# Linear attention feeding a residual MLP: load order of w_tok, its transposes, and the shape of the first q.kv products

## The chip, the cores and the metric

The kernel runs on one core of one Trainium2 chip. The metric is the device time of one execution in microseconds (us), taken as the median of several executions. The core has a matrix engine (TensorE, PE in the profile, its weight loads PEld), a vector engine (VectorE, DVE), a scalar engine (ScalarE, ACT), GpSimd (POOL), SyncE (SP), which here only issues transfers, and 16 DMA engines.

## The reference

Eight heads of linear attention are normalised, laid side by side as 512 channels, and go through a token-mixing and a channel-mixing layer:

```python
# q, k, v: (8, 8, 576, 64) fp32
kv  = np.einsum('bhsd,bhse->bhde', k, v)
o   = np.einsum('bhsd,bhde->bhse', q, kv)
o   = o / np.sqrt(np.mean(o * o, axis=-1, keepdims=True) + 1e-06) * g_norm
x   = o.transpose(0, 2, 1, 3).reshape(8, 576, 512)

a1  = alpha1 * x + beta1
tok = np.einsum('ts,bsd->btd', w_tok, a1)        # w_tok: (576, 576)
u   = x + lam * tok
a2  = alpha2 * u + beta2
ch  = np.maximum(a2 @ w_ch1, 0.0) @ w_ch2        # 512 -> 2048 -> 512
return u + lam * ch
```

## The kernel before

**A program that plans itself.** The code first lists all operations with what they read and write (`P.op`). Then `Prog.schedule` plays them through in planned time: each operation has a planned cost, each SP load a planned landing, and each engine takes, when it is free, the ready operation of lowest `pri`. Where an operation names several engines (a dict of costs), the planner chooses one. The result is a fixed order of instructions for each engine, written with semaphore waits. On the chip every engine follows its list; nothing is reordered at run time. `hasten` gives all ancestors of the first expansion matmuls a `pri` below -980, so the prologue goes ahead of everything else. The loads of the prologue are issued by SP strictly in the order of the list `order`; a load that waits for its buffer holds back those behind it.

When the planner finds nothing for PE before the first expansion matmul, it puts in a warm-up matmul (L1333) on zeros. `idle` says how soon after one the next may follow.

**PSUM.** There are eight banks of 512 fp32. `ptile(n)` is a tile of one or two banks, and `place` picks the banks.

**Tokens.** Token s of the 576 is written as 9 x (s // 9) + c. Column c of nine gives 64 tokens, so a group of two columns fills 128 partitions; the ninth column gives a half-filled group, and those of two batches share a tile (`xtl`).

**Prologue, batch 0.** Heads come in two halves (k0, v0, q0 and k1, v1, q1). For each half:
- `kv_groups` (L590): k.v in fp32, 64x64 products, four at a time in the quarters of the array; copies to `kvr` in fp32r, with the same values in the lower and the upper 64 partitions;
- `qt_groups` (L558, L551): q transposed by PE into `qtr` and `qtrt`;
- `qkv_groups` (L680, `f32`): q.kv in fp32r. Two token columns lie in the two 64-partition halves of `qtr`; a product has 64 rows, and lower and upper halves alternate, each writing a PSUM bank of its own;
- the norm: square (L709), sum (L711), root (L714), reciprocal (L717), scaling into `xm` (L733); then `rt` = x * alpha1 * lam * g (L737) and x * g (L740).

Batch 1 takes the same fp32r path with all eight heads at once; the later batches take a bf16 path with a high and a low part (L670, L385).

**w_tok.** `wt_groups` needs w_tok transposed, with rows and columns in the order of the tokens above. Five row groups of w_tok are loaded (four of 128 rows, one of 64). `cast` (L1109 on) reads every ninth column of a group and writes 512 reordered bf16 columns, `cast_tail` the ninth column's 64. Four PE transposes a group (L1136) and five for the tail (L1158) follow, copies into `wt`, and `sums` (L1188): the row sums of w_tok, two rows of which stand in `wt` for beta1 * lam (constant rows, stored into `rt` by DMAs that ScalarE issues, L1052).

`tok_half` (L800) is the token mixing of batch 0 by half of the channels, with its residual sum at L811. `ut_first` (L832) transposes u for the first expansion matmuls (L932, then L901). From there PE runs through expansion (L901 for even batches, L916 for odd), contraction (L966), token mixing of the next batch (L766, and L779 for the last 64 tokens of two batches), with the attention of a later batch between. The 64 last rows of w_tok serve only L779.

**Weights.** `load_w` brings w1 in four pieces (w0 to w3) and w2 in four (w4 to w7) through three buffers `stg`; w1 is cast (L1254), w2 scaled by `lam` (L1267). `bias_groups` (L1211) multiplies beta2 with w1. Bk, Bv, Bq in `order` are the loads of batch 1. `params` prepares rows such as `e1_bc`; its transpose L1033 waits for alpha2 and beta2, which ScalarE's queue loads.

Of the kernel before, what the change touches and what calls it, by code (L numbers as in the profile page):

```python
# [36 lines left out]
class PTile:  # L37
# [4 lines left out]
    def __init__(self, prog, n):  # L42
        self.prog, self.n, self.bank, self.ops = prog, n, None, []

    def ap(self, parts=slice(0, 128)):
        return self.prog.ps[parts, self.bank:self.bank + self.n, :]
# [5 lines left out]
class Prog:  # L52
# [79 lines left out]
    def schedule(self):  # L132
# [25 lines left out]
        def place(tile, t):  # L158
            if tile.n == 2:
                c = [b for b in (0, 2, 4, 6) if bank_ok(b, t) and bank_ok(b + 1, t)]  # L160
                if not c:
                    return None
                return min(c, key=lambda b: max(bank_since(b), bank_since(b + 1)))
            c = [b for b in range(8) if bank_ok(b, t)]
            if tile.spare:
                c += [b for b in range(8) if owner[b] is not None and owner[b].spare]
                return max(c, key=lambda b: (owner[b] is not None and owner[b].spare, b),
                           default=None)
            if not c:
                return None  # L170
            return min(c, key=lambda b: (bank_ok(b ^ 1, t), bank_since(b)))
# [43 lines left out]
        while left:  # L215
            progressed = False
            for e, q in queues.items():
                while q and free[e] <= t + 1e-9:
# [5 lines left out]
                    if e == "PE" and cold > 1.2:  # L224
                        cands = ([o for o in q[:2 * self.pe_window] if not o.cold]
                                 + [o for o in cands if o.cold])
                    for o in cands:
                        if not ready(o, t):
                            continue
                        if port_free > t + 0.1 and shared(o, e):  # L230
# [11 lines left out]
                    if pick is None and e == "PE" and first and t >= idle:  # L242
# [5 lines left out]
                        if ready(pick, t):  # L248
                            left += 1
                            q.append(pick)  # L250
                            idle = t + (1.0 if t < 9 else 2.0) * pick.cost
# [12 lines left out]
                    for tile in pick.alloc:  # L264
                        tile.bank = place(tile, t)
                        for b in range(tile.bank, tile.bank + tile.n):
# [8 lines left out]
                    if pick.lat is not None:  # L275
                        if e == "SP":
                            dma_free = max(dma_free, t + (1.9 if t < 3 else 1.25)) + pick.lat
# [114 lines left out]
def bass_transnormer_attn__then__resmlp_affine_kernel(  # L392
# [15 lines left out]
    with ExitStack() as stack:  # L408
# [24 lines left out]
        with nc.sbuf_tensor("kvr", [128, NH, DH], F32R) as kvr, \  # L433
                nc.sbuf_tensor("qtrt", [128, NH, 128], F32R) as qtrt:
# [13 lines left out]
        wt = sb("wt", [128, 6, S], BF16)  # L448
        w1 = sb("w1", [128, 4, FF], BF16)
# [7 lines left out]
        wst = hst[:, 0:2880].rearrange("p (c s) -> p c s", c=5)  # L457
        wsb = hst[:, 2880:4480].bitcast(BF16).rearrange("p (c s) -> p c s", c=5)
        smask = hst[:, 4480:4544].bitcast(BF16)
# [82 lines left out]
        def qt_groups(b):  # L542

            def group(a, m):
# [23 lines left out]
                else:  # L568
                    o = qtrt[0:64, 4 * a:4 * a + 4, lo:lo + 64]
# [800 lines left out]
```

## Time and profile before

| | us |
|---|---|
| median of 4 runs | 369.08 |
| lowest, highest | 367.11, 370.59 |
| profiled execution: its time | 370.06 |
| profiled execution: its span | 368.2 |
| PE busy | 356.9 (97%) |
| PEld, DVE, ACT, POOL busy | 211.2, 204.2, 146.9, 122.6 |
| first expansion matmul (L932) starts | 36.1 |
| first contraction matmul (L966) starts | 64.4 |
| last product ends | 364.7 |

The span is what the profiler saw from the first instruction to the last; the execution's time holds a little more around it (370.06 - 368.2 = 1.9). The kernel has a prologue of 36 us, in which loads, w_tok and the attention of batch 0 lie beside each other on all engines, and a long part in which PE works without a break. A time saved in the prologue counts if PE can start its long part sooner and then finds its operands.

### The profile page before, as it was taken

How to read it: one execution, taken by the hardware profiler on the slowest of the kernel's cores; microseconds unless marked ns; L12 is line 12 of the kernel's file. 1: busy time of each engine (PE TensorE's matmuls, PEld its weight loads, DVE VectorE, ACT ScalarE, POOL GpSimd, SP SyncE). 2: the span in 40 equal slices, each digit the busy share in tenths (PEclk: the TensorE clock that was granted, in tenths of full speed). 3: DMA queues.
4: the chain of work that ended last, by engine and by line, in shares of the span. 5: the costliest groups of instructions: out<-in, count | busy, mean ns of one | idle time of the engine just before them, and what ended most of it. 6: DMA issues, size and time to landing. Idle time of an engine off the chain costs nothing.

```text
span 368.2 us, 7917 instructions
## 1 busy us (share of the span) xinstructions
PE 356.9 (97%) x3542; PEld 211.2 (57%) x3302; DVE 204.2 (55%) x305; ACT 146.9 (40%) x254; POOL 122.6 (33%) x100
## 2 busy tenths in 40 slices
PE   6999959999999999999999999999999999999996
PEld 4878736447764464447754554447754554447644
DVE  1376729975397259752676179743874189720021
ACT  1588216404852048305860059006740157007600
POOL 4478464670055002730183004820572005400000
PEclk9989989999999999999999999999999999999999
DMA  8998997008694669387937685477946710341023
GB/s 286 352 385 266 341 373 279 2 0 124 155 352 80 120 115 378 76 107 120 318 112 116 130 258 214 84 103 113 372 72 112 150 31 0 64 94 30 0 59 85
DMA packets 67558, 59.17 MB, mean 161 GB/s; under 512 B 45552, under 2 KB 45828, under 8 KB 67524
## 3 DMA queue, kind: packets, MB, share of 16 engines
q1 hardware_dynamic: 67440, 58.65, 60.1%
q8 instruction: 27, 0.44, 0.5%
q14 instruction: 7, 0.06, 0.1%
q10 hardware_dynamic: 84, 0.02, 0.0%
HBM read 38.60 MB, written 9.44 MB: 130 GB/s over the span
## 4 chain that ended last, share of the span: by engine, by line
PE 93%; POOL 1%; DMA 1%; issue 1%; DVE 1%; ACTq 0%; ACT 0%; POOLq 0%
PE ps L966 34%; PE ps L916 19%; PE ps L901 14%; PE ps L766 8%; PE ps L590 5%; PE ps L385 2%; PE ps L670 2%; PE ps L680 2%; DMA w<-in_moe_beta_dram 1%; PE ps L558 1%; PE ps L779 1%; PE ps L1333 1%; PE ps L932 1%; POOL rt L737 1%; POOL xm L740 1%
## 5 line engine op out<-in xcount | busy, mean ns | idle before, releaser
L966 PE MATMUL ps<-w,ht 128*128 128x512 bf16 (+1 forms) x592 | 129.0, 373 | 0.0
L890 ACT ACTIVATE ht<-ps,bias 128x640 bf16<-128x640 f32 (+2 forms) x101 | 74.9, 743 | 50.9 <-PE ps L916 37.2
L966 PEld LDWEIGHTS ps<-w,ht 128*128 128x128 bf16 x592 | 56.7, 98 | 64.5 <-issue 1.6
L916 PE MATMUL ps<-a2t,w 128*128 128x320 bf16 x512 | 71.5, 299 | 0.0
L740 POOL TENSOR_TENSOR xm<-xm,g_bc 128x1024 f32<-128x1024 f32 (+1 forms) x16 | 33.3, 2082 | 109.5 <-DVE rt L737 109.1
L916 PEld LDWEIGHTS ps<-a2t,w 128*128 128x128 bf16 x512 | 49.5, 98 | 20.1
L901 PE MATMUL ps<-a2t,w 128*128 128x512 bf16 x240 | 55.7, 383 | 0.0
L977 DVE TENSOR_TENSOR xm<-ps,xm 128x512 f32<-128x512 f32 (+1 forms) x33 | 22.0, 673 | 55.7 <-PE ps L966 55.6
L621 ACT ACTIVATE kvd<-ps 64x256 bf16<-64x256 f32 x24 | 9.1, 378 | 97.1 <-PE ps L590 96.9
L711 DVE TENSOR_REDUCE small<-sq 128x16 f32<-128x1024 f32 (+3 forms) x27 | 24.9, 930 | 22.8 <-ACT sq L709 22.6
L901 PEld LDWEIGHTS ps<-a2t,w 128*128 128x128 bf16 x240 | 22.8, 99 | 25.4 <-issue 0.6
L766 PE MATMUL ps<-rt,wt 128*128 128x512 bf16 x140 | 31.4, 379 | 0.0
L891 DVE TENSOR_SCALAR ht<-ps,bias 128x512 bf16<-128x512 f32 (+2 forms) x31 | 22.2, 724 | 12.6 <-PE ps L901 6.4
L522 POOL TENSOR_TENSOR qs<-qf,qs 128x512 bf16<-128x512 f32 x13 | 16.5, 1270 | 28.2 <-ACT qs L481 27.5
L709 ACT ACTIVATE sq<-ps 128x1024 f32<-128x1024 f32 (+3 forms) x27 | 21.2, 797 | 11.3 <-PE ps L385 8.2
L749 DVE TENSOR_TENSOR xm<-ps,xm 128x512 f32<-128x512 f32 x28 | 19.1, 689 | 8.7 <-PE ps L766 7.1
L590 PE MATMUL ps<-vf,kf 64*64 64x64 f32 x1152 | 20.1, 226 | 3.9 <-issue 3.9
L766 PEld LDWEIGHTS ps<-rt,wt 128*128 128x128 bf16 x140 | 13.7, 98 | 16.5
L590 PEld LDWEIGHTS ps<-vf,kf 64*64 64x64 f32 x1152 | 18.7, 141 | 7.2 <-issue 7.0
L977 DVE TENSOR_TENSOR xtl<-ps,xtl 128x512 f32<-128x512 f32 x4 | 2.8, 692 | 35.5 <-PE ps L966 35.5
L751 POOL TENSOR_TENSOR a2b<-xm,a_bc 128x512 bf16<-128x512 f32 x12 | 18.2, 1513 | 8.7 <-DVE xm L749 8.4
L733 DVE TENSOR_TENSOR xm<-ps,small 128x1024 f32<-128x1024 f32 (+1 forms) x18 | 19.7, 1096 | 0.2
(101 smaller groups left out, 339.8 us busy)
## 6 DMA issues: line engine op xcount, KB each, us to landing
stg<-in_moe_w_ch_dram SPq DMA_DIRECT2D x8, 1024.0 KB, 13.2
kf<-in_k_dram SPq DMA_DIRECT2D x7, 1152.0 KB, 6.1
vf<-in_v_dram SPq DMA_DIRECT2D x7, 1152.0 KB, 9.6
qf<-in_q_dram SPq DMA_DIRECT2D x7, 1152.0 KB, 11.0
out_dram<-xm SPq DMA_DIRECT2D x62, 128.0 KB, 2.4
kf<-in_k_dram SPq DMA_DIRECT2D x2, 576.0 KB, 5.5
vf<-in_v_dram SPq DMA_DIRECT2D x2, 576.0 KB, 7.1
qf<-in_q_dram SPq DMA_DIRECT2D x2, 576.0 KB, 8.6
```

Source lines behind the costliest of these rows:

```text
L590: m = e.matmul(t.ap(slice(64 * i, 64 * i + 64))[:, y, 64 * x_:64 * x_ + 64], kf[rows, x, c], vf[rows, x, c], start=(c == 0), stop=(c == 8) ...
L709: P.op("ACT", act_us(64 * m), lambda e: e.activation(both(sqv), raw(), ACT.Square), r=[t], w=[("sq", sqs)])
L711: P.op("DVE", dve_us(64 * m), lambda e: e.tensor_reduce(out=smv, in_=sqv, axis=AX.X, op=ALU.add), r=[("sq", sqs)], w=[("sm", sms)], pri=-20)
L733: P.op("DVE", dve_us(64 * m), lambda e: e.tensor_tensor(out=x3, in0=raw(), in1=inv(), op=ALU.mult), r=[t, ("sm", sms)], w=xk, pri=-200)
L740: P.op(dve_pool(64 * m) if b < 2 else "POOL", pool_us(64 * m), lambda e: e.tensor_tensor(out=x3, in0=x3, in1=gb, op=ALU.mult), r=xk + ["g" ...
L766: m = e.matmul(t.flat(), wt[:, sc if sc < 4 else 4 + b % 2, 128 * c:128 * c + 128], rt[:, rs(b, sc), :], start=(sc == 0), stop=(sc == 4))
L890: return e.activation(dst, src(), ACT.Relu, bias=bi)
L891: return e.tensor_scalar(out=dst, in0=src(), scalar1=bi, scalar2=0.0, op0=ALU.add, op1=ALU.max)
L901: m = e.matmul(t.flat(), w1[:, dj, 128 * fj:128 * fj + 128], a2t[:, dj, 0:512], start=(dj == 0), stop=(dj == 3))
L916: m = e.matmul(t.ap()[:, i, 0:320], w1[:, dj, 128 * fj:128 * fj + 128], a2t[:, dj, 320 * i:320 * i + 320], start=(dj == 0), stop=(dj == 3))
L966: m = e.matmul(t.flat()[:, 0:m_], ht[:, fj, 128 * c:128 * c + 128], w2[:, fj, lo:hi], start=(fj == 0), stop=(fj == 15))
L977: P.op("DVE", dve_us(m_), lambda e: e.tensor_tensor(out=x, in0=t.flat()[:, 0:m_], in1=x, op=ALU.add), r=[t] + keys, w=keys)
```

## The change

- **w_tok in three parts.** `wt_groups(r)` takes row groups 0 and 1, then 2 and 3, then the last 64 rows. The loads t1 and t2 go later in `order`, t2 far later, into buffers of its own (`wst4`, `wsb4`). Token mixing waits for the part that it reads.
- **Plain casts.** `cast` writes 576 columns in their own order, `cast_tail` is gone. The column picks move to PE: weights are read with a stride of nine, and multiplied with the identity, two 64-column products in the two halves of the array, into fp32.
- **Three tails, three sums** instead of one tail and two sums.
- **q.kv block-diagonal.** `kvr` is 128 wide, zero off the diagonal, and `qtr` is used with all 128 partitions. A group of batch 0 has four products of 128 columns instead of eight of 64; one of batch 1 has 16 of 64 columns and 128 rows instead of 16 of 64 and 64. A group of batch 0 takes one PSUM bank instead of two. `qtrt` holds the two halves of heads in its two halves of partitions.
- **Constant rows** are stored by SP, just behind w0.
- **Parameter transpose** L1033 comes after the k.v product of half 0.
- **Planner.** Other planned costs and landings, warm-up matmuls twice as dense between planned times 9 and 26, another choice of banks, and a rule that holds back PE operations which would take the last pair of neighbouring banks from a waiting urgent one.
- **Order of loads**: Bq goes ahead of lam, a2 and w4.

```diff
             if tile.n == 2:
-                c = [b for b in (0, 2, 4, 6) if bank_ok(b, t) and bank_ok(b + 1, t)]
-                if not c:
-                    return None
-                return min(c, key=lambda b: max(bank_since(b), bank_since(b + 1)))
+                c = [b for b in c if b + 1 in c]
+                return (lambda b: [b, b + 1])(min(c, key=lambda b: (
+                    sum(bank_ok(x, t) for x in (b - 1, b + 2) if 0 <= x < 8),
+                    max(bank_since(b), bank_since(b + 1))))) if c else None
...
                         if not ready(o, t):
+                            if e == "PE" and o.pri < -980.0:
+                                held = max([held] + [x.n for x in o.alloc])
                             continue
+                        if held > 1 and o.alloc:
...
-                            idle = t + (1.0 if t < 9 else 2.0) * pick.cost
+                            idle = t + (1.0 if t < 26 else 2.0) * pick.cost
...
-                            dma_free = max(dma_free, t + (1.9 if t < 3 else 1.25)) + pick.lat
+                            dma_free = max(dma_free, t + (2.5 if t < 3 else 1.25)) + pick.lat
...
-        with nc.sbuf_tensor("kvr", [128, NH, DH], F32R) as kvr, \
-                nc.sbuf_tensor("qtrt", [128, NH, 128], F32R) as qtrt:
+        with nc.sbuf_tensor("kvr", [128, NH, 128], F32R) as kvr, \
+                nc.sbuf_tensor("qtrt", [128, 4, 128], F32R) as qtrt:
...
-                t = P.ptile(nc_)
+                t = P.ptile(64 * m // 512 or 1)
...
                 def f32(e):
-                    for h in range(h0, hs.stop):
-                        for i in range(nc_):
-                            r_ = slice(64 * i, 64 * i + 64)
-                            w = (qtr[r_, h, 2 * cs[0]:2 * cs[0] + 2, :].rearrange(
-                                "p k s -> p (k s)") if nc_ > 1 else qtrt[r_, h, :])
-                            mm = e.matmul(t.ap()[:, i, 64 * (h - h0):64 * (h - h0) + 64], w,
-                                          kvr[r_, h, :], start=True, stop=True)
+                    if nc_ > 1:
+                        for h in range(nh):
+                            w = qtr[:, h0 + h, 2 * cs[0]:2 * cs[0] + 2, :].rearrange(
+                                "p k s -> p (k s)")
+                            for x in range(1 if nh < 8 else 2):
+                                y = slice(0, 128) if nh < 8 else slice(64 * x, 64 * x + 64)
+                                o = (t.flat().rearrange("p (c h d) -> p c h d", c=2, d=64)[
+                                    :, :, h, :] if nh < 8 else t.cols(64 * (nh * x + h), 64))
+                                mm = e.matmul(o, w, kvr[:, h0 + h, y], start=True, stop=True)
...
             P.op("PE", 0.15, lambda e: e.transpose(t.flat()[:, 0:8], pcol[:], ident[0:8, 0:8]),
-                 r=["ident", ("pc", 0), ("pc", 1)], w=[t])
+                 r=["ident", ("pc", 0), ("pc", 1)], w=[t], after=P.lastw[("kvp", 0)])
...
-                    P.op("AQ", 0.35, lambda e, i=i, p=p, c=c: e.dma_start(
+                    P.op("SP", 0.6, lambda e, i=i, p=p, c=c: e.dma_start(
                         rt[p + i:p + i + 1, c, :].rearrange("o (j p) -> o j p", p=128),
-                        ebf[:, i, :]), r=["ebh", "ebl", "rtz"], w=[("rtc", x, i)], dma_us=0.05)
+                        ebf[:, i, :]), r=["ebh", "ebl", "rtz"], w=[("rtc", x, i)], dma_us=0.05,
+                        at=sp["w0"] + 0.1 + 0.01 * (2 * x + i))
...
-        order = ["k0", "v0", "q0", "k1", "t0", "t1", "t2", "v1",
-                 "q1", "w0", "g", "w1", "w2", "Bk", "Bv", "w3", "lam", "a2", "w4",
-                 "Bq", "w5", "w6", "w7"]
+        order = ["k0", "v0", "q0", "k1", "t0", "v1", "q1", "t1",
+                 "w0", "g", "w1", "w2", "Bk", "Bv", "w3", "Bq", "lam", "a2", "t2", "w4",
+                 "w5", "w6", "w7"]
...
-        P.op("DVE", 0.6, lambda e: e.memset(qtrt[0:64, :, 64:128].bitcast(F32), 0.0), w=["qtp"])
+        P.op("DVE", 0.6, lambda e: e.memset(qtrt[:].bitcast(F32), 0.0), w=["qtp"])
+        P.op("DVE", 0.6, lambda e: e.memset(kvr[:].bitcast(F32), 0.0), w=["kvz"])
...
                 def f(e):
                     for sc in range(4):
-                        m = e.transpose(
-                            t.flat().bitcast(BF16)[:, 128 * sc:128 * sc + rr],
-                            wsb[0:rr, tc, 128 * sc:128 * sc + 128], identb[0:rr, 0:rr])
+                        for z in range(2):
+                            c = 4 * (sc % 2) + 2 * z + sc // 2
+                            m = e.matmul(t.flat(slice(64 * z, 64 * z + 64))[
+                                :, 128 * sc:128 * sc + rr], b16(tc)[:, c:576:9],
+                                identb[0:rr, 0:rr], start=True, stop=True,
+                                tile_position=(0, 64 * z))
                     return m
-                P.op("PE", 0.28, f, r=["identb", ("wsb", tc)], w=[t])
+                P.op("PE", 0.45, f, r=["identb", ("wsb", tc)], w=[t], cold=True)
...
-        run([wt_groups()])
+        run([wt_groups(r) for r in range(3)])
```

## The prediction

> **What bounds the kernel now.** I read the page's 40 slices first. TensorE (PE) is busy in nearly every slice; only the first, two near the start and one at about 46 us are not full. So the end moves only if the PE's own work changes or one of those holes does.
>
> ```profile
> span 368.2 us, 7917 instructions
> PE   6999959999999999999999999999999999999996
> PEclk9989989999999999999999999999999999999999
> DMA  8998997008694669387937685477946710341023
> q8 instruction: 27, 0.44, 0.5%
> ```
>
> Then the chain that ended last, for the prologue, that is until the first expansion matmuls (L932, at 36.24 us). Columns: start, length, what.
>
> ```profile
> 7.95 0.27 PE ps L1033
> 9.61 2.13 PE ps L590 x72
> ...
> 19.32 0.75 PE ps L1158 x5
> 20.07 0.54 PE ps L1136 x4
> 20.61 1.27 PE ps L590 x72
> ...
> 22.97 0.22 PE ps L551 x2
> ...
> 23.52 0.56 PE ps L680 x8
> 24.41 1.01 PE ps L680 x12
> ...
> 32.87 1.28 POOL xm L740
> 34.17 0.44 DVE xm L811
> ```
>
> Two things to see. The first k.v product (L590, half 0) starts at 9.6, although its inputs landed at 6.05 (issued 1.25, 4.8 later, by the DMA view): the PE's order puts the parameter transpose L1033 ahead of it, which waits for beta. And the product of half 1 starts at 20.6, although v1 landed at 15.5 (issued 6.12, 9.4 later): ahead of it stand w_tok transposes L1158 and L1136, which wait for strided casts on ScalarE until about 19.
>
> Last, the PE's timeline around the hole, with the stages beside it (columns: stage, length, then busy time and count for PE, PEld, DVE, ACT, POOL, then granted clock, DMA share, GB/s).
>
> ```profile
> 43.92 2.21 PE L590 MATMUL ps<-vf,kf 64*64 64x64 f32 x135
> 50.00 0.38 PE L590 MATMUL ps<-vf,kf 64*64 64x64 f32 x9 [3.88 <-issue]
> 46.20:50.00 3.80, 0.00 (x0) 0.00 (x0) 0.00 (x0) 0.00 (x0) 1.25 (x1) 1.00 1.05 382
> 50.00:55.00 5.00, 5.00 (x29) 3.31 (x30) 2.29 (x4) 1.73 (x4) 4.69 (x5) 0.66 1.03 365
> ```
>
> The PE stops inside one group, with no wait. The instruction queue q8 moved 27 packets, 0.44 MB, and PE plus PEld have 3542 + 3302 = 6844 instructions: about 256 a packet. In windows of the DMA view one packet falls at 38 to 41 us, the next only at 47 to 48, with the DMA engines full (share 1.05). The L590 group is 288 instructions in some 2.2 us, so it eats a block faster than the next arrives. The hole costs 3.88 us and the half clock after it (1 - 0.66) x 5 = 1.7: **5.6 us**. The Trainium skill, "Runtime: NRT & Kernel Launch", section "Instruction fetch mechanics", says instructions come in 16 KiB blocks and that crossing one is "mostly hidden". The size agrees with 0.44 MB / 27; the hiding fails here. By the page no change could touch these 5.6 us; by the trace a change that shifts instruction counts can.
>
> **The change, part by part.**
>
> *Loads.* t1 (2 x 288 KB) and t2 (144 KB) move behind v1 and q1. Landings by the DMA view: first t piece 10.2, t2 14.1, v1 15.5, q1 17.65. Four pieces cost about 1 us each, so v1 should land near 12.5, q1 near 14.6, then t1 at 16.7. w0 comes 0.6 sooner (t2's part).
>
> *Half 0.* L1033 moves behind L590, so L590 starts at 6.1 to 6.9 instead of 9.6: some 3 us. The four constant-row stores leave ScalarE's queue (8.72 to 11.24, 2.52 us). That cost nothing, as ScalarE's first copy waited for L590 until 11.81; with L590 done near 9 it would have cost, so the move is needed. On SP they stand behind w0 and wait for the GpSimd cast that ends at 8.7, then take about 0.5 each: g, w1 and all behind them are issued some 3 us later (w1 at 11.4, not 8.38). Hidden by 12 us of loads queued ahead (w0 landed at 20.5); without that cover w1 is 3 us late.
>
> *Half 1.* q1 at 14.6, L558 and L551 1.1 us (0.87 + 0.22): the first L680 near 16.0 instead of 23.52. From there the trace needs 36.24 - 23.52 = 12.7 us to L932. To that I add 2.5, because w_tok rows 1, casts, copies and sums, and GpSimd's work of half 0 (L737, L740) now fall into the same stretch: L932 near 31.2, a gain of 5.0.
>
> *Cross-check by engine time.* From 11.7 to 36.2 DVE, ACT and POOL are busy 16.1 + 19.7 + 17.2 = 53.0 of 3 x 24.5, or 72%. The strided casts cost 1.10 + 1.11 + 1.45 on POOL and 1.10 + 0.64 + 1.10 on ACT, 6.5 us; four plain ones at 0.67 (rows w<-stg: 0.61 on ACT, 0.65 on POOL, a ninth more for 576 columns) are 2.7. The late 64 rows take 1.0 of copies away; four half-width evictions of the sums for two add 0.3. That is 4.5 less, 2.1 us at 72% of three engines, plus the 3.0 earlier start: 5.1. Both agree; I take **-5.0**, with 2 and 8 as ends (2: the PE's written order waits for another late cast; 8: no contention, 36.24 - (16.0 + 12.7) = 7.5, and a little clock). On the clock, the row first: the PE is busy throughout 11.7 to 20.5, yet granted 0.82. The skill's "TensorE: Matmul & The Clock Gate", Part 4, says that transpose mode does not count as busy; by that page the identity matmuls might return up to 0.18 x 8.8 = 1.6 us, by the row nothing tells transposes from the 64-row products. I count none.
>
> *Block-diagonal q.kv, batch 1.* Sixteen pairs take 1.90 and eight single products 1.01 (rows L680 at 56.94 and 59.81). With 1.90 = 16u + f and 1.01 = 8u + f, u = 0.111, f = 0.12: two half-height products together cost what one does alone. The new form has 32 full-height ones of the same width: 32u + f = 3.68, or **+1.8** on a PE that has no idle there. Low end 0 (if full height runs at half the time, as transposes of 128 columns do in 0.109 each). I take 1.8, as the single 64-column products are nearest. In batch 0 four of 128 columns replace eight: between 4 x 0.11, equal, and double, +0.45 a group; both lie in the prologue, inside the 2 to 8.
>
> *Late rows.* Eight small matmuls at 0.055 (0.22 for four, L1136), a transpose, five sums: **+0.8**, now after the first expansion where the PE is full; 0 if in a hole, 1.1 by the cold rows. Before, they hid under the wait for L740. The two larger memsets fall into DVE's idle time before 4.47, 0; if DVE had none, 1 us.
>
> *Banks, held-back ops, fillers.* From 50 us to the last product the PE has no hole over 0.1, so a new order gains nothing there; it may lose. I take 0, up to +2.
>
> *The instruction hole.* Fewer L680 before it (-32 instructions), more w_tok matmuls (+22), and more warm-up matmuls by the denser rule below 26 (0 to +76, by the PE's idle time in the shorter prologue). The block that ran dry began some 38 instructions into L590 (288, dry at the 270th, a block of 256, plus waits); a shift of -10 to +66 leaves that block almost entirely inside L590 and L1211. I therefore keep the hole.
>
> **Sum** against the profiled execution, 370.06 (span 368.2): -5.0 + 1.8 + 0.8 = -2.4, so 367.7. The median of four is 369.08, so **366.7**.
>
> **Rivals.**
>
> *The hole goes (0.27).* If the boundary slides by a hundred instructions or more, slow L901 matmuls cover the fetch: 366.7 - 5.6 = 361.1. For: the count is uncertain and Bq's earlier load may reorder that stretch. Against: 288 instructions always cross a boundary.
>
> *The prologue does not shorten (0.14).* The three vector engines stay the limit and half 1 waits on them: a gain of 1 at most, 366.7 + 4 = 370.7. For: GpSimd is busy 13.72 of 15.7 us from 20.5 to 36.2. Against: it idles 3.87 at 15.7 to 19.6.
>
> *w2 becomes the bound (0.12), slower.* Bq (1152 KB, 3 us at 390 GB/s) and t2 now stand ahead of w4, and w7's slot is w4's. The last scaling of w2 ends on POOL at 74.25; the PE reads it at 76.09, a margin of 1.85. If the loads keep their pace, it ends at 74.25 + 3.4 = 77.6 while the PE, 2.4 ahead, asks at 73.7: 3.9 of waiting, and 1.7 of clock, so 366.7 + 5.6 = 372.3. It decides once that scaling ends later than 73.7. Against: from 30 to 40 us the loads had holes (239 and 221 GB/s) behind w3's wait for its slot; earlier casts close them and give the 3.4 back.
>
> **Chances.** The forecast, shorter prologue with the hole kept, has 0.42 and runs by its own costs from 363.5 to 369.5; 0.05 is left for the rest. One per cent, 3.7 us, is about what a measurement here tells from no change. Faster: 0.27 of the first rival, 0.14 of the forecast's low end, 0.02: 0.43. Slower: 0.11 of w2, 0.03 of the second rival: 0.14. Same: 0.43. The range, 359.5 to 371.0, reaches below the first rival and up to the second.
>
> **What would show it.** L932 near 31; L590 of half 0 before 7 and of half 1 near 13; L680 of batch 1 at about 0.11 a product; a gap without a wait inside or just after L590 of batch 1 and a half clock behind it. A gap under 1 us there proves the first rival; L932 after 35 the second; a PE wait ended by L1267 the third.

## The result and the profile after

The changed kernel takes 369.55 us (median of 45 runs, 368.18 to 370.06), the kernel before 368.54 in the runs beside it (71 runs, 365.92 to 371.10). The ratio is 1.0018 with an interval from 1.0007 to 1.0029: a loss of 0.3 to 1.1 us, where 2.4 us of gain were forecast. The profiled execution of the changed kernel took 369.08 us, 1.0 less than the profiled execution that the forecast was summed against. Both statements are true, and the gap between them is a large part of this case.

The slices and the instruction queue of the changed kernel, from its page:

```profile
span 367.3 us, 7961 instructions
PE   8999699999999999999999999999999999999995
PEclk9999989999999999999999999999999999999999
DMA  7999939008694789488906684468935610331023
q8 instruction: 27, 0.44, 0.5%
```

The first slice is fuller (8 against 6). The hole is still there, now as the 6 in the fifth slice (36.7 to 45.9 us), and so is the lower clock in the slice behind it (8); the clock's dip in the third slice is gone. The chain of the prologue (start, length, what):

```profile
8.47 1.09 PE ps L572 x8
...
13.47 1.53 PE ps L1347 x13
15.00 1.21 PE ps L604 x72
16.21 1.02 PE ps L572 x8
17.23 0.22 PE ps L565 x2
17.45 0.61 PE ps L1156 x8
...
18.28 0.46 PE ps L1156 x7
18.75 0.43 PE ps L1347 x3
19.18 0.40 PE ps L697 x4
...
32.53 3.49 PE ps L956 x32
```

The k.v product of half 1 (L604, L590 before) starts at 15.0 instead of 20.6, the expansion (L956, L932 before) at 32.53 instead of 36.24. The PE's timeline of the changed kernel, the first k.v product and then the rows around the hole (start, length, engine, line, count, idle before it):

```profile
6.70 1.28 PE L604 MATMUL ps<-vf,kf 64*64 64x64 f32 x72
...
40.18 2.08 PE L604 MATMUL ps<-vf,kf 64*64 64x64 f32 x124
46.38 0.56 PE L604 MATMUL ps<-vf,kf 64*64 64x64 f32 x19 [4.11 <-issue]
...
47.34 1.97 PE L572 MATMUL ps<-ident,qf 128*128 128x128 f32 x8
...
51.96 3.74 PE L697 MATMUL ps<-kvr,qtr 128*128 128x64 f32 x32
```

The hole is 4.11 us; behind it the eight transposes L572 take 1.97 us, where the next eight (at 50.05) take 1.07: the granted clock is 0.50 from 46.7 to 50.1. The 32 full-height products L697 take 3.74, where the 32 half-height ones of before took 1.97:

```profile
56.87 1.97 PE L680 MATMUL ps<-kvr,qtr 64*128 64x64 f32 x32
```

### The profile page after: what moved, and what is told of

The parts are those of the page before. It is cut to its first block, busy times and chain, and to the rows that moved or that the text cites. A ratio compares the mean times of both kernels' runs of the same rounds, so it can differ in the third digit from the quotient of the medians.

```text
span 367.3 us, 7961 instructions
## 1 busy us (share of the span) xinstructions
PE 356.7 (97%) x3566; PEld 213.7 (58%) x3326; DVE 210.5 (57%) x308; ACT 146.5 (40%) x257; POOL 114.8 (31%) x95
## 4 chain that ended last, share of the span: by engine, by line
PE 88%; DVE 6%; DMA 2%; issue 2%; POOL 1%; ACT 1%; SPq 0%; POOLq 0%; DVEq 0%
PE ps L990 32%; PE ps L940 19%; PE ps L925 13%; PE ps L789 7%; PE ps L604 5%; PE ps L684 2%; PE ps L397 2%; DMA qf<-in_q_dram 2%; DVE rt L761 2%; PE ps L697 1%; PE ps L572 1%; PE ps L802 1%; PE ps L956 1%; DVE xm L757 1%; DVE w L1281 1%
## 5 line engine op out<-in xcount | busy, mean ns | idle before, releaser
L990 PE MATMUL ps<-w,ht 128*128 128x512 bf16 (+1 forms) x592 | 128.9, 373 | 0.0
L990 PEld LDWEIGHTS ps<-w,ht 128*128 128x128 bf16 x592 | 56.8, 98 | 64.0 <-issue 1.2
L914 ACT ACTIVATE ht<-ps,bias 128x640 bf16<-128x640 f32 (+2 forms) x99 | 73.3, 741 | 46.7 <-PE ps L940 38.7
L764 POOL TENSOR_TENSOR xm<-xm,g_bc 128x1024 f32<-128x1024 f32 (+1 forms) x17 | 35.7, 2098 | 117.2 <-DVE rt L761 115.2
L925 PE MATMUL ps<-a2t,w 128*128 128x512 bf16 x240 | 54.5, 379 | 0.0
L915 DVE TENSOR_SCALAR ht<-ps,bias 128x512 bf16<-128x512 f32 (+2 forms) x33 | 24.1, 738 | 11.6 <-PE ps L925 5.2
L604 PE MATMUL ps<-vf,kf 64*64 64x64 f32 x1152 | 19.3, 220 | 4.1 <-issue 4.1
L604 PEld LDWEIGHTS ps<-vf,kf 64*64 64x64 f32 x1152 | 17.8, 135 | 7.2 <-issue 7.0
L775 POOL TENSOR_TENSOR a2b<-xm,a_bc 128x512 bf16<-128x512 f32 x12 | 17.1, 1425 | 13.5 <-DVE xm L773 9.9
```

Of the source, the lines that this page charges most:

```text
L604: m = e.matmul(t.ap(slice(64 * i, 64 * i + 64))[:, y, 64 * x_:64 * x_ + 64], kf[rows, x, c], vf[rows, x, c], start=(c == 0), stop=(c == 8) ...
L764: P.op(dve_pool(64 * m) if b < 2 else "POOL", pool_us(64 * m), lambda e: e.tensor_tensor(out=x3, in0=x3, in1=gb, op=ALU.mult), r=xk + ["g" ...
L914: return e.activation(dst, src(), ACT.Relu, bias=bi)
L915: return e.tensor_scalar(out=dst, in0=src(), scalar1=bi, scalar2=0.0, op0=ALU.add, op1=ALU.max)
L925: m = e.matmul(t.flat(), w1[:, dj, 128 * fj:128 * fj + 128], a2t[:, dj, 0:512], start=(dj == 0), stop=(dj == 3))
L990: m = e.matmul(t.flat()[:, 0:m_], ht[:, fj, 128 * c:128 * c + 128], w2[:, fj, lo:hi], start=(fj == 0), stop=(fj == 15))
```

## The experiments

In the tables below every start is that of the line's first row in the PE's timeline. "Product" is the k.v product of batch 1, "contraction" the first matmul of L966 (L990 after). "Half clock" is a granted clock of 0.5. The runs were made in sets on different chips, each beside runs of the kernel before, and a ratio is to those. The kernel before with the shift, measured in two sets, has medians 1.2 us apart (362.45 and 363.67): a difference between medians of two sets is no surer than that.

### Is the reference itself steady, and does the hole cost what was said?

**The kernel before, unchanged** (`b_same`). 

> The kernel before, unchanged, to see how its profile varies. Its times spread from 366 to 371 us, while the profiled execution of the prediction's page took 370.06. Theory (the part of the spread lies in the instruction hole and in the half clock behind it): another profile shows the hole in the k.v product of batch 1 again, at the same instruction, but of another length or with another number of half-clock windows, and the time moves with these two alone. Rival (the spread is in DMA and the prologue): the start of the first expansion matmuls moves by over 0.5 us and the hole does not.

Measured: 368.9 us, ratio 0.9988 (0.9963 to 1.0013). No change. The profile has the hole again, 3.55 instead of 3.88, with one stretch of half clock behind it; the start of the expansion also moved, by 0.6 us (36.10 to 36.69), so neither theory nor rival holds whole.

**An instruction shift alone**, in both kernels (`a_shift`, `b_shift`). Of the warm-up matmuls ahead of the first k.v product 17 are each cut into eight of 32 columns, seven of which keep their weights, 119 instructions more:

```diff
-            return e.matmul(t.flat()[:, 0:256], wz[:, 0:128], wz[:], start=True, stop=True)
+            warmed.append(t)
+            if len(warmed) > 17:
+                return e.matmul(t.flat()[:, 0:256], wz[:, 0:128], wz[:], start=True, stop=True)
+            m = e.matmul(t.flat()[:, 0:32], wz[:, 0:128], wz[:, 0:32], start=True, stop=True)
+            for i in range(1, 8):
+                m = P.matmul_held(t.flat()[:, 32 * i:32 * i + 32],
+                                  wz[:, 0:128], wz[:, 0:32], True, True)
+            return m
```

> The changed kernel with 119 more PE instructions before the first k.v product: 17 early warm-up matmuls of 256 columns are cut into eight of 32 columns on the same weights; the PE's time for them is the same. Theory (the hole is a late instruction block): the block boundary moves by 119 instructions, out of the k.v product's danger zone, the 4.1 us hole shrinks below 1 us and the half-clock window behind it goes: 369.5 - 4 to 6 = 363.5 to 365.5. Rival (the hole belongs to that place in time, a saturated DMA, not to the instruction count): the hole stays at 4 us and the time at 369.5.

> The kernel before with the same 119 instructions more. Theory: its hole of 3.9 us goes too, 368.5 - 4 to 6 = 362.5 to 364.5, so the hole cost both kernels alike and the change did not touch it. Rival: the time stays at 368.5.

Measured: the changed kernel 365.48, ratio 0.9899 (0.9874 to 0.9923), 4.1 below its own median of 369.55; the kernel before 362.45, ratio 0.9838 (0.9805 to 0.9872), 6.2 below its 368.68 in that set (4.9 when it was measured again, `b_shift_2` below). In both profiles the hole is gone. So the hole follows the count of instructions, that is, where the block boundary lies; it costs both kernels, and the forecast was right that a shift could take it away and that this change would not. In the changed kernel the PE then shows something new (timeline, then two stretches by engine: stretch, length, busy PE, PEld, DVE, ACT, POOL, granted clock, DMA share, GB/s):

```profile
45.06 0.41 PE L565 MATMUL ps<-ident,qf 128*64 128x128 f32 x2 [0.67 <-DVE wt L496]
...
47.18 3.74 PE L697 MATMUL ps<-kvr,qtr 128*128 128x64 f32 x32
```

```profile
47.70:51.10 3.40, 3.40 (x30) 3.17 (x30) 3.40 (x5) 1.30 (x3) 2.73 (x3) 0.96 0.83 254
51.10:54.50 3.40, 3.40 (x12) 1.66 (x10) 2.17 (x2) 1.74 (x3) 2.60 (x3) 0.53 1.04 393
```

The PE is busy throughout, from 47.2 to 50.9 with nothing but full-height products, and then runs at half clock for 3.4 us. Not every execution does: five of the twelve runs have a granted clock of 0.998 or more, so no whole stretch of 3.4 us at half clock, and took 363.96 to 364.94; those with 0.991 to 0.995 took 365.37 to 366.19.

### The full-height products

**The changed kernel with the products of batch 1 in pairs of 64 rows again** (`a_pairs`):

```diff
-                                mm = e.matmul(o, w, kvr[:, h0 + h, y], start=True, stop=True)
+                                r_ = y if nh == 8 else slice(0, 128)
+                                mm = e.matmul(o, w[r_], kvr[r_, h0 + h, y], start=True, stop=True)
```

> The changed kernel with the 16 products of a group of batch 1 in pairs of 64 partitions again (as many instructions, same planned order). Theory: 32 full-height products take 32 x 0.111 + 0.12 = 3.7 us, 16 pairs 1.9 us, and the PE has no idle time behind them, so the kernel gains 1.8 us against the changed kernel: 367.7. Rival (the vector engines set the start of token mixing of batch 1, which began at 70.2 in both profiles): the 1.8 us come back as waiting and the time stays within 0.5 us of 369.5.

Measured: 367.45, ratio 0.9970 (0.9951 to 0.9989), 2.1 below the changed kernel (1.8 by the two ratios), as the theory had it; the hole (3.56) and the half clock behind it stay. The timeline has the products back at their old length:

```profile
51.84 1.97 PE L698 MATMUL ps<-kvr,qtr 64*128 64x64 f32 x32
```

**The kernel before with the shift and full-height products** (`b_full_shift`):

```diff
-                            r_ = slice(64 * i, 64 * i + 64)
+                            r_ = slice(0, 128) if nh == 8 and nc_ > 1 else slice(64 * i, 64 * i + 64)
```

> Kernel before, 119 instructions more, and the q.kv products of batch 1 with all 128 partitions instead of pairs of 64 (the two token columns are then summed, so batch 1 is computed wrongly; the amount of work is that of the changed kernel). Theory: 1.8 us more on the PE, and a half clock window (1.7 us) behind 3.6 us of full-height products: 362.4 + 1.8 to 3.5 = 364.2 to 366. Rival (pairs and full height cost alike once the hole is gone, as the weights' load is the limit): 362.4.

Measured: 367.83, ratio 0.9969 (0.9934 to 1.0004), 5.4 above the shift alone by the medians and 4.8 by the ratios, more than expected. The products take 3.84 instead of 1.97, 1.9 more; then the clock is at half for 6.8 us, without a hole ahead of it:

```profile
51.10:54.50 3.40, 3.33 (x29) 3.09 (x30) 3.40 (x4) 1.35 (x2) 3.24 (x3) 0.97 1.07 392
54.50:57.90 3.40, 3.40 (x13) 2.20 (x12) 2.89 (x3) 1.38 (x2) 3.24 (x3) 0.50 1.04 386
```

The runs tell the two costs apart. The two of ten with a granted clock of 0.994 and 0.995 took 363.86 and 364.30, some 1.3 to 2.2 above the four of the shift alone at 0.995 (362.09 to 362.58); the other eight, at 0.981 to 0.986, took 366.29 to 368.86. So full height costs its length, about 1.8, and where it fills a whole stretch of 3.4 us it can cost clock as well. In the changed kernel itself no second half-clock stretch follows the products (51.96 to 55.70).

**The changed kernel with pairs and shift** (`a_pairs_shift`, both diffs above).

> Changed kernel, 119 instructions more before the first k.v product and the products of batch 1 in pairs. Theory (full height costs twice: 1.8 us of PE time, and a 3.4 us window of nothing but full-height fp32r products after which the clock was halved once more at 51.1 us in the run with the shift alone): both go, 365.5 - 1.8 - 1.7 = 362.0, with no half clock between 46 and 56 us. Rival (the half clock comes from the fp32 transposes and late w_tok rows that stand together there, not from the products): half clock stays, 363.7.

Measured: 363.52, ratio 0.9892 (0.9858 to 0.9926). No hole, and no half clock before the end, as the theory had it; but the time is the rival's, 1.5 above the theory's 362.0. That is not below the kernel before with the shift.

### The parameter transpose and ScalarE's stores

**The kernel before with the shift, and L1033 behind the first k.v product** (`b_l1033_shift`), while ScalarE keeps the constant-row stores:

```diff
-                 r=["ident", ("pc", 0), ("pc", 1)], w=[t])
+                 r=["ident", ("pc", 0), ("pc", 1)], w=[t], after=P.lastw[("kvp", 0)])
```

> Kernel before, 119 instructions more, and the parameter transpose put behind the k.v product of half 0, alone. Theory (in the prologue the vector engines, the late casts and half 1 decide): the k.v product of half 0 starts some 2.5 us sooner, the first expansion matmul by under 1 us, time 361.5 to 362.4. Rival (the PE's first wait shifts the whole prologue): first expansion 2 to 3 us sooner, 359.5 to 360.5.

Measured: 366.37, ratio 0.9941 (0.9914 to 0.9968), 3.9 above the shift alone (2.7 above its second measurement); theory and rival both missed. The product starts 3 us sooner, at 6.59, at full clock (1.28 us instead of 2.20). But ScalarE must copy its result, and its queue stands in the four stores until 11.30:

```profile
8.78 2.52 ACTq L1052 DMA_DIRECT2D rt<-w  x4
11.35 0.57 ACT L481 ACTIVATE kvr<-ps 64x128 fp32r<-64x128 f32 x2 [8.21 <-issue]
```

```profile
12.57 0.91 PE L680 MATMUL ps<-kvr,qtr 64*128 64x64 f32 x8 [2.79 <-ACT qtr L481]
```

PE idles 2.79 us, the clock is at half for the next 10.2 us, and the expansion starts at 38.4 instead of 36.4. So the move of L1033 alone costs as long as the stores stand in ScalarE's queue, as the prediction had it. That it pays with the stores on SP is not shown by itself: no run makes these two moves and nothing else.

### The late rows

**Pairs and shift, with t2 loaded right behind t1** (`a_t2_pairs_shift`; three warm-ups cut up, 21 instructions):

```diff
-        order = ["k0", "v0", "q0", "k1", "t0", "v1", "q1", "t1",
-                 "w0", "g", "w1", "w2", "Bk", "Bv", "w3", "Bq", "lam", "a2", "t2", "w4",
+        order = ["k0", "v0", "q0", "k1", "t0", "v1", "q1", "t1", "t2",
+                 "w0", "g", "w1", "w2", "Bk", "Bv", "w3", "Bq", "lam", "a2", "w4",
```

> As a_pairs_shift, with the last 64 rows of w_tok loaded right behind t1 (they then go into holes of the prologue; the planner also moves the k.v product of batch 1 ahead of the first expansion, and only 21 instructions are added so that the block boundary lies 100 instructions into that product). Theory: the late rows cost about 1.3 us behind the first expansion (0.7 of waiting for a copy, the rest matmuls), so 360.5 to 361.5. Rival: the k.v product of 2.1 us now delays the first expansion by as much as is saved, or the hole comes back: 362 to 366.

Measured: 367.96, ratio 0.9991 (0.9963 to 1.0019). A miss, outside both ranges: the planner puts the product of batch 1 ahead of the expansion, and in the second eight pairs of L698 PE waited 2.08 us for a `qtr` copy that stood behind w2's scalings (L1282) on VectorE, and the clock was at half for 10.2 us. So a second version holds that product back and uses the full shift (`a_t2_late`), run together with both shifted kernels again:

```diff
-                P.op("PE", 0.2 + 1.06 * np_, f, cold=True, w=[t, ("kvp", hs.start)],
+                cnt[b] = P.op("PE", 0.2 + 1.06 * np_, f, cold=True, w=[t, ("kvp", hs.start)],
...
-        P.hasten(set(first_ch1))
+        P.hasten(set(first_ch1)) or cnt[1].deps.update(first_ch1[:8])
```

> The change without the late instruction block and without full-height products in batch 1, again, so that it stands beside the next three on one chip. Theory: without these two the rest of the change still loses about 1 us to the kernel before with the same shift, because the late rows and the order after them (about 2.2 us) cost more than the earlier start gives (about 1.6 us at equal clock): 363.0 to 364.0, 0.5 to 1.5 above the next kernel. Rival: the rest of the change is a gain of 1.6 us or more and the earlier difference was chance: 361.5 to 362.

> The kernel before with 119 more PE instructions ahead of the first k.v product, again, on the same chip as the kernel above. Both theories: 362.0 to 363.0.

> The change with pairs and shift, its last 64 rows of w_tok loaded right behind the other 512, and the k.v product of batch 1 held behind the first eight expansion matmul groups. Theory: the rows' transposes and picks (14 matmuls, their copies and the 0.6 us wait for them) now lie in front of the expansion in time that PE fills with warm-ups anyway, so the stretch from the expansion to the contraction shortens by about 1.1 us, the expansion starts up to 0.5 us later for the added load, and the contractions keep their old order or not: 362.0 to 363.0, 0.5 to 1.5 below the first kernel of this set. Rival: the added load delays everything behind it by its 0.8 us and more, and the expansion starts that much later: 363.5 to 365.

Measured: pairs and shift 363.51 (0.9864, 0.9835 to 0.9893); the kernel before with the shift 363.67 (0.9865, 0.9837 to 0.9894); t2 early 364.69 (0.9894, 0.9859 to 0.9928). On this chip the first two are level, so the first theory failed: with the hole and the full height gone, the rest of the change is worth nothing that shows (the two intervals leave room for about 1 us either way). Early late-rows were no gain either: their work left the stretch behind the expansion, and a wait of 1.43 us came in its place, L572 for a `qtr` copy of VectorE.

These profiles also hint at what an earlier start is worth once the hole is gone. Two executions of the kernel before with the shift, one in each set, started the expansion at 36.36 and 33.69, 2.67 apart; their times, 364.42 and 363.67, are 0.75 apart. The late one has no PE wait from 32 to 72 us. The early one has these (waiting engine, its line, what ended the wait: total, times, longest):

```profile
PE ps L558 <- DVE w L1267: 0.5, 1, 0.5
PE ps L766 <- DVE rt L737: 0.5, 1, 0.5
PE ps L901 <- DVE ht L891: 0.4, 1, 0.4
```

All are waits for VectorE, 1.4 us of the 1.9 that the early start loses; one of them is for a scaling of w2. The two executions of pairs and shift are alike: 1.12 apart at the start (32.70 and 33.82), 0.18 at the end.

Where the 2.67 us come from can be read from the same two profiles: they are there when the second k.v product starts (20.66 and 17.89). At L1033, which waits for beta, it is 0.6 (8.06 and 7.48). From there PE has no wait until the product, but the late execution lies at half clock for 10.2 us up to 21.2 us and the early one for 3.4, so that the same rows take longer, as these of b_shift and b_shift_2:

```profile
11.97 1.91 PE L558 MATMUL ps<-ident,qf 128*128 128x128 f32 x8
11.27 1.04 PE L558 MATMUL ps<-ident,qf 128*128 128x128 f32 x8
```

### The warm-up rule, and whether the start is one of executions

**The kernel before with the shift and the changed kernel's denser warm-ups** (`b_dense_shift`):

```diff
-                            idle = t + (1.0 if t < 9 else 2.0) * pick.cost
+                            idle = t + (1.0 if t < 26 else 2.0) * pick.cost
```

> The kernel before with the shift (13 tiles instead of 17 cut up, since there are 13 more warm-ups) and the changed kernel's rule for warm-ups: the next one follows after 1.0 instead of 2.0 of its cost until 26 us of planned time. Theory: idle stretches of PE in the prologue are what lets the clock fall to half there in some executions of the kernel before, and these executions are its slower ones; with the denser warm-ups the profile shows no half clock before the expansion, which starts at 34.5 to 35.5 instead of 36.6, and the times lie at 361.5 to 362.3 with a narrower spread. Rival: the clock in the prologue has another cause, or costs nothing there: half-clock windows as before, expansion at 36.3 to 36.8, 362.3 to 363.

Measured: 364.73, ratio 0.9912 (0.9878 to 0.9947). A miss, outside both ranges: a half-clock stretch at 17 us stayed, and 13 warm-ups instead of 7 ran 2.80 us at that clock ahead of L1158; the expansion started at 37.0.

**Three more profiles of the kernel before, one more of the changed kernel.**

> The kernel before, unchanged, for one more profiled execution. Theory: the profiled execution that the prediction was worked out against started its expansion late (36.34 us) because PE ran its first products at half clock and met another half-clock window at 17.6, and other executions of the same kernel start it near 34, as one of two profiles of the kernel before with the shift did (33.93 against 36.60). So of these three profiles at least one starts the expansion below 35 us, and its time is below 369. Rival: the shift itself moved the start, and the kernel before always starts its expansion at 36 to 37 us.

> The same again. Theory: an expansion start between 33.5 and 37, following the half-clock windows ahead of it. Rival: 36 to 37.

> The same again. Theory: an expansion start between 33.5 and 37, following the half-clock windows ahead of it. Rival: 36 to 37.

> The changed kernel, unchanged, for one more profiled execution. Theory: its first products run at full clock, so its start varies less: 32.4 to 34.1, time 368.2 to 370.1. Rival: its start varies as widely as that of the kernel before, up to 35 or more.

| profile | expansion | product | hole | half clock behind the hole | contraction | span | time |
|---|---|---|---|---|---|---|---|
| before (the forecast's) | 36.10 | 43.92 | 3.88 | 3.4 us | 64.43 | 368.2 | 370.06 |
| b_same | 36.69 | 44.51 | 3.55 | 3.4 us | 64.55 | 368.3 | 370.18 |
| b_again_1 | 36.06 | 43.87 | 3.52 | 6.8 us | 64.92 | 368.7 | 370.57 |
| b_again_2 | 36.00 | 43.81 | 3.62 | none | 62.38 | 366.2 | 367.95 |
| b_again_3 | 35.75 | 43.57 | 3.66 | none | 62.18 | 365.9 | 367.75 |
| after | 32.37 | 40.18 | 4.11 | 3.4 us | 62.42 | 367.3 | 369.08 |
| after_again | 32.66 | 40.47 | 3.56 | 3.4 us | 62.48 | 367.2 | 369.02 |

The theory of the start fell: the kernel before starts its expansion at 35.8 to 36.7 in all five, the changed one at 32.4 and 32.7, so the 3.1 to 4.3 us are a real difference between the kernels. Part of it is clock: in all five profiles of before the first eight L558 take 1.68 to 1.91 us, in the two of the changed kernel L572 there takes 1.09. The changed kernel's own expectation held (start 32.66, time 369.02). What differs most between executions of the kernel before lies behind the hole. In b_again_2 the same matmuls, behind a hole of the same length, run at full clock:

```profile
43.81 2.20 PE L590 MATMUL ps<-vf,kf 64*64 64x64 f32 x135
49.64 0.38 PE L590 MATMUL ps<-vf,kf 64*64 64x64 f32 x9 [3.62 <-issue]
49.96 1.04 PE L901 MATMUL ps<-a2t,w 128*128 128x512 bf16 x4
50.83 1.04 PE L558 MATMUL ps<-ident,qf 128*128 128x128 f32 x8
```

```profile
49.64:53.05 3.41, 3.41 (x30) 2.46 (x31) 2.35 (x5) 1.73 (x4) 3.25 (x3) 1.00 1.05 370
```

and in the changed kernel (the `after` profile) at half:

```profile
46.90:50.31 3.41, 3.41 (x30) 3.10 (x26) 1.66 (x5) 2.05 (x7) 2.41 (x3) 0.53 0.20 73
```

**Does it matter what stands behind the hole?** (`a_t2_hole`: `a_t2_late` with 32 warm-ups cut up, so that the boundary lies in the product again.)

> The kernel a_t2_late with 32 instead of 17 warm-ups cut up, so that the instruction boundary lies again inside the first half of L604 of batch 1 as in the changed kernel, but behind that product come 512-column matmuls (L926), as in the kernel before, and not the small late w_tok matmuls. Theory: the changed kernel always has a half-clock window behind the hole because of the small matmuls there; here a hole of 3.5 to 4.1 us comes back without the window, the stretch from the product's end to the first contraction is 12.6 to 13.2 us, and the time is 365.0 to 366.5. Rival: what stands behind the hole does not matter; the window stays, the stretch is 14.2 us or more, and the time is 367 to 368.5.

Measured: 367.98, ratio 0.9992 (0.9962 to 1.0022), the rival's time. The profile has a hole of 4.26 us and 6.8 us of half clock behind it, with 512-column matmuls there:

```profile
49.01 0.92 PE L604 MATMUL ps<-vf,kf 64*64 64x64 f32 x22 [4.26 <-issue]
49.86 1.89 PE L926 MATMUL ps<-a2t,w 128*128 128x512 bf16 x4
```

So small matmuls behind the hole are not needed for the half clock. What goes with it can be read from the nine profiles with the hole. The half clock begins and ends on a grid of 3.413 us that lies differently in each execution. I laid the grid of each execution over the starts and lengths of its PE rows; it cuts the hole in two or three. This is the PE's idle time in the windows that were entered at full clock, and the clock of the window after each:

| profile | idle in the windows that the hole touches, us | clock of the next window |
|---|---|---|
| before | 1.92, 1.96 | full, half |
| b_again_1 | 2.09 | half |
| b_again_2 | 1.88, 1.75 | full, full |
| b_again_3 | 1.84, 1.83 | full, full |
| after_again | 1.46, 2.11 | full, half |
| after | 1.02, 3.09 | full, half |
| a_pairs | 0.52, 3.04 | full, half |
| b_same | 0.02, 3.41 | full, half |
| a_t2_hole | 0.08, 3.41 | full, half |

Every window of this table with 1.96 us idle or more is followed by half clock, none with 1.92 or less. A hole of 3.6 us escapes if the grid cuts it nearly in the middle. Idle time is not the only way to half clock, though: laid over all nineteen profiles up to 70 us, the grid shows 14 windows with 1.10 us idle or less that were entered at full clock and followed by half. Eleven lie in the prologue, with no idle time at all, and hold the first q.kv products (`before`: 13.9 to 17.3 us, with L680 and L1024); two are those of the full-height products above; the last, in a_t2_pairs_shift, holds 1.10 us of idle time and half-height products. What brings the clock down in those of the prologue was not tried. The Trainium skill, "TensorE: Matmul & The Clock Gate", Part 1, tells of a free-running window of 3413 ns and of a return to half clock after an idle window; the length and the free running agree with the grid here, while 1.96 idle of 3.41 was already enough.

## Why the prediction was wrong

**Against one execution it was off by 1.4; against the median by 2.9.** Its sum was 370.06 - 2.4 = 367.7 for the profiled execution; 369.08 came. From that sum it took off the 1.0 by which the four shown runs of before lie below its profile. The median of the changed kernel, though, lies 0.5 above its own profile: 1.4 + 1.0 + 0.5 = 2.9.

**Three terms of the sum failed.** The start of the expansion gained 3.3 us, not 5.0. The half clock behind the hole, counted as equal on both sides, cost the changed kernel about 1.2 more. And the stretch from the contraction to the end, entered as 0, cost 1.0. Together that is 3.9 us; the late rows, which cost 0.35 less than forecast, leave 3.5, the way from -2.4 to +1.07 in the table below.

**The half clock is a matter of the execution.** In the profile that the sum went by the kernel before had half clock behind the hole, and its median over all runs is 1.5 lower. The step "I therefore keep the hole" kept the 1.7 us of half clock with it on both sides. But on the side of before it comes in three of five profiles (without it the times were 367.75 and 367.95), and in both profiles of the changed kernel it is there. The granted clock of single runs agrees: in the runs of the kernel before beside the experiments, those at 0.994 took 365.7 to 367.9 us and those at 0.977 took 370.5 to 371.0. None of the 45 runs of the changed kernel was below 368.18 or had a granted clock above 0.995, which is what one stretch of 3.4 us at half clock leaves of 367 us. So each had at least one such stretch; that it always lay behind the hole is not shown, and why the grid spares the changed kernel less often is open.

**Where the time goes** can be summed from b_again_2, which had no half clock behind the hole, to after_again, 367.95 to 369.02, +1.07:

| step | forecast | measured | from |
|---|---|---|---|
| start of the expansion | -5.0 | -3.3 | 36.00 to 32.66 |
| expansion to contraction: full-height products | +1.8 | +1.8 | 29.82 us after, 28.03 in a_pairs |
| the same: late rows | +0.8 | about +0.45 | 22.96 in a_pairs_shift_2, 22.51 in b_shift, neither with a hole or a wait |
| the same: half clock behind the hole | 0 (on both sides) | about +1.2 | the rest of 28.03 - 26.38 |
| contraction to the end of the span | 0 (up to +2) | +1.0 | 303.78 to 304.76 |

The measured column adds to +1.15, against +1.07. The parts of the stretch from the expansion to the contraction are differences between single profiles, and the half clock is what the other two leave.

- **The start, mis-sized by 1.7.** The mechanism was right: L604 of half 0 started before 7 and that of half 1 came 5.6 us sooner, though at 15.0 and not near 13. The first L697 of half 1 came at 19.18, not near 16.0. q1 landed at about 15.0 (forecast 14.6) and v1 near 13.4 (12.5), but warm-ups filled PE up to 15.0, and behind the q transposes PE's order put the w_tok transposes L1156 and three warm-ups (17.45 to 19.18 in the chain) ahead of L697, while ScalarE copied `qtr` behind two w_tok casts (15.73 to 17.07). So the crowding came one stage earlier than assumed and cost more than its allowance of 2.5: 3.2 us up to L697, while from L697 to the expansion it took 13.4 us, not much over the 12.7 that the trace of before needed.
- **The products: right**, 3.74 against a forecast of 3.68. The rate of before (16u + f, 8u + f) was enough to price a shape that the trace did not hold.
- **The late rows: half of what was taken.** Loading them early gave nothing (a_t2_late), since PE then waited 1.43 us for VectorE.
- **Behind the contraction: "a new order gains nothing there; it may lose"** was right in sign, and the 1.0 is within the bound given, but it was entered as 0. Of it 0.5 us lies between the first and the last contraction matmul, and 0.4 behind the last of them. No run isolates an edit that does it, so the cause of this term stays open.
- **The hole: right that it stays.** It came 11 products earlier in the group (after 124 instead of 135), 22 instructions with their weight loads, inside the shift of -10 to +66 that was counted. The rival that it goes would have given 361.1; the shift alone gives 365.5 in the changed kernel, in part since the full-height products then can bring a half clock of their own and PE meets VectorE's wait (0.67).
- **w2 as the bound did not come as drawn** (a PE wait ended by a scaling of w2 ahead of L966). The last scaling of w2 did end later than the 73.7 named as the sign, at 74.7, but PE came to the next contraction at 76.0, as before (76.1), and did not wait. Its milder form is what b_shift_2 shows: as soon as the hole is gone, the early PE waits for VectorE, one piece of it for a w2 scaling (0.5 us).

What stays open: what brings half clock into the prologue where PE has no idle time; whether executions of the changed kernel ever escape the half clock behind the hole; and which edit costs the 1.0 us behind the start of the contraction.

## What to carry to other kernels

Sum a change against a profile only after asking which parts of that profile belong to the kernel and which to the execution: a half-clock stretch behind a hole of about its own length can be there in one run and not in the next, and here it was as large as the change's whole effect. A hole inside one group, with no wait and one late packet on the instruction queue, is worth trying to move before anything else: 119 more instructions took 4.9 to 6.2 us off the kernel before, more than the whole rewrite of its prologue was forecast to give. And an earlier start counts only as far as the next engine keeps up; read that engine's slack first.

## What the runs showed of the hardware

- **The instruction block that comes late costs 3.5 to 4.3 us in nine profiles**, always inside the 64x64 product of batch 1, while the DMA engines are full (share 1.05 over the hole in the kernel before, 0.94 in the changed one).
- **The clock follows windows of 3.413 us.** In the nine profiles with the hole, a window there that was entered at full clock and idle for 1.96 us or more was followed by half clock, and one idle for 1.92 or less was not.
- **A busy PE is not safe from it.** In a_shift and b_full_shift a window of 3.4 us filled with full-height fp32r products of 64 columns, with 0 to 0.07 us of idle time, was followed by half clock. The same number of products in pairs of half height takes 1.97 us and so cannot fill a window; behind it the clock stayed full in a_pairs_shift. In eleven profiles a window of the prologue without idle time was followed by half clock too.
- **Half clock where PE starts.** In the kernel before PE waits 2.2 us for beta ahead of L1033, and the product behind it takes 2.20 us; in the changed kernel, without that wait, 1.28. In b_same, whose clock record reaches back that far, the window of that wait (2.36 us idle) is followed by half clock from 9.2 us, and the product takes 2.13.
